# RWKV-6 scan and squared-ReLU MLP on one core: w in two-token rows for four chunks, the decay sum moved into the state update's bank, a split last tile, and a new order

## The chip, the cores and the metric

The kernel runs on one core of a Trainium2 chip. Five queues run side by side, each in its own order: TensorE (PE), VectorE (DVE), ScalarE (ACT), GpSimd (POOL) and SyncE (SP), which here only starts DMA transfers. The metric is the device time of one execution in microseconds, as the median of several runs.

## The reference

Four sequences, eight heads, 768 tokens, 48 channels per head. A linear recurrence with a decay `w` per channel and token is followed by a two-layer MLP over all 3072 tokens:

```
for t in range(S):
    cur = einsum('bhd,bhe->bhde', u[None] * kt, vt)
    y[:, :, t] = einsum('bhd,bhde->bhe', rt, state + cur)
    state = wt[:, :, :, None] * state + einsum('bhd,bhe->bhde', kt, vt)
x = y.transpose(0, 2, 1, 3).reshape(B * S, H * D)      # 3072 x 384
r = maximum(x @ w_in, 0.0)                             # w_in 384 x 2048
out = (r * r) @ w_out                                  # w_out 2048 x 384
```

## The kernel before

**Tiling.** The tokens are cut into 24 chunks ("steps") of 128 tokens, six for each sequence. A step is done for all eight heads at once, tokens on the partitions. The MLP works on 12 blocks of two steps each: `m1` is the first layer (a group `m1:i:g` makes two of the 16 slices of 128 hidden channels, 6 matmuls of 256 columns), `rl` the ReLU on ACT, `gt` the square on DVE, `m2` the second layer (a quarter `m2:i:mt:q` is 4 matmuls of 384 columns, and four quarters make an output tile of 128 tokens), `os` its copy out of PSUM, `store` the transfer out.

**One step of the scan.** `ld` brings r, k, v and w of the step, each one transfer of 192 KB. `lw` takes the logarithm of w on ACT. `cum` is a matmul with a triangular matrix, which sums the logarithms over the tokens into a tile `cp` of two PSUM banks. `exp` turns it into decay factors on ACT, and `rd` multiplies r and k with them on DVE. `tr` and `rkt` transpose the result (PE, then DVE), `p` and `pm` make the masked scores, `su` the chunk's contribution to the state, `ts` adds it to the state (DVE), and `sn` multiplies the state with the decay of the whole chunk, `a_c` (POOL). `y` makes the outputs, `ku`, `qp`, `q`, `vq` the term with `u`, `ysb` adds it, and `yt` and `xt` transpose into `xT`, the input of the MLP.

**What the change touches.** `a_c` needs the sum of the logarithms over the chunk. Five small matmuls put it beside the running sum, in the bank of `cp` (lines 190 to 195), and ACT takes its exponential at the end of `exp` (lines 207 to 209). For the first `V5 = 8` steps `cum` has a second matmul with a negated triangular matrix (line 198), and `exp` is one activation of 768 elements (line 203). Later steps use only the first matmul, two activations of 384 (lines 205 and 206), and the pair `rw` (ACT, line 160) and `kw` (POOL, line 164), which rescales k.

**PSUM.** There are eight banks: `cp` has two and is used in turn by `cum` and `p`; `y` has one; `tr` has one, which is used in turn by the transposes of `tr`, by `su` and by `yt`; four `mm` banks are for the MLP and for `warm`, matmuls on zeros that compute nothing.

**The order.** Everything is put into its queue by a list of words written out by a planner beforehand, `order`, that is read from left to right. A word such as `su:4` puts the instructions of `su` for step 4 into the queues. Within an engine the order of the list holds; between engines semaphores do the waiting. The list begins so:

```python
    order = """
        ld:0:w ld:0:r warm:6:0 ld:1:w ld:0:k lw:0 ld:0:u cum:0 ld:0:v warm:4:1 ld:1:v lw:1 ld:1:r exp:0 ub ld:1:k rd:0
        ...
```

`warm:6:0` is six matmuls into bank 0. `ld:n:I` and `ld:n:O` are the eighths of the two MLP weight matrices (384 KB each, lines 90 and 96); `cast` copies them into bf16 (line 104), even groups on ACT and odd groups on DVE.

Of the kernel before, what the change touches and what calls it, by code (L numbers as in the profile page):

```python
# [16 lines left out]
def kernel(  # L17
# [11 lines left out]
    nc = tc.nc  # L29
# [14 lines left out]
    A_IN = 7  # L44

# [26 lines left out]
    def load_step(step, part):  # L72
        b, c = divmod(step, NCH)
        if part in "wv":
            raw[part, step] = a_in.tile([C, H, D], FP32, name=part + "_raw")
            load_one(raw[part, step][:], w if part == "w" else v, b, c)
        else:
            if ("rk", step) not in raw:
                raw["rk", step] = a_in.tile([C, 2, H, D], FP32, name="rk_raw")
            i = "rk".index(part)  # L80
            load_one(raw["rk", step][:, i], (r, k)[i], b, c)
# [26 lines left out]
    u_row = consts.tile([1, H, D], FP32)  # L108
# [3 lines left out]
    def load_u():  # L112
        nc.sync.dma_start(out=u_row[:], in_=u[None])

    def ub_():
        ps = tiles["ub"] = ps_y_pool.tile([C, H, D], FP32, name="y")
        nc.tensor.matmul(ps[:], ones_row[:], u_row[:], start=True, stop=True)
# [3 lines left out]

    tri_strict = consts.tile([C, C], BF16)
# [14 lines left out]
    V5 = 8  # L137
    NLW = 3
# [15 lines left out]
    def lw_(s):  # L154
        lw = tiles["lw", s] = lw_bufs[s % NLW]
        nc.scalar.activation(lw[:, :, 0:D], raw["w", s][:], AF.Ln)  # L156
# [43 lines left out]
    def exp_(s):  # L200
# [6 lines left out]
        if s % NCH < NCH - 1:  # L207
            a_c = tiles["a_c", s] = a_small.tile([C, HP, 2], FP32, name="a_c")
            nc.scalar.activation(a_c[:], cs[:, 0, DM:DM + 2 * HP].rearrange("p (a e) -> p a e", e=2), AF.Exp)  # L209
# [18 lines left out]
    def p_(s):  # L228
        rkT = tiles["rkT", s]
        ps_p = tiles["p", s] = ps_cp.tile([C, 2, 512], FP32, name="cp")  # L230
        for p in range(HP):
            for e in range(2):
                rows = slice(e * DP, (e + 1) * DP)
                nc.tensor.matmul(ps_p[:, e, p * C:(p + 1) * C], rkT[rows, 1, p, :],  # L234
                                 rkT[rows, 0, p, :], start=True, stop=True)
# [7 lines left out]

    def su_(s):
        rdec, v_bf = tiles["rdec", s], tiles["v", s]
        ps_su = tiles["su", s] = ps_tr_pool.tile([C, HP, 2, D], FP32, name="tr")
        for p in range(HP):
            nc.tensor.matmul(ps_su[:, p], rdec[:, 1, 2 * p:2 * p + 2, :],
                             v_bf[:, 2 * p:2 * p + 2, :], start=True, stop=True)

    def ts_(s):
        ps_su = tiles.pop(("su", s))
        ts = tiles["ts", s] = a_mid.tile([C, HP, 2, D], FP32, name="t_state")
        if s % NCH == 0:
            nc.vector.tensor_copy(ts[:], ps_su[:])
        else:
            nc.vector.tensor_add(ts[:], tiles["S", s][:], ps_su[:])  # L257
# [76 lines left out]

    def warm_(n, b):
# [4 lines left out]
    def ld_(n, x):  # L340
        {"i": load_wi, "o": load_wo}.get(x.lower(), lambda g: load_u() if x == "u" else load_step(g, x))(n)

    run = dict(rw=rw_, kw=kw_, lw=lw_, v=v_, cum=cum_, exp=exp_, rd=rd_, tr=tr_, rkt=rkt_, p=p_, pm=pm_, su=su_, ts=ts_,
# [4 lines left out]
        ld:0:w ld:0:r warm:6:0 ld:1:w ld:0:k lw:0 ld:0:u cum:0 ld:0:v warm:4:1 ld:1:v lw:1 ld:1:r exp:0 ub ld:1:k rd:0  # L348
        warm:1:2 uc ld:2:w cum:1 v:0 ku:0 exp:1 su:0 ld:3:w warm:3:3 ts:0 v:1 tr:0 sn:0 ld:2:v warm:9:0 rd:1 ku:1 ld:2:r
        rkt:0 qp:0 lw:2 ld:2:k p:0 qp:1 tr:1 pm:0 ld:0:I warm:4:1 ld:3:r ld:4:w rkt:1 cum:2 y:0 exp:2 su:1 ld:3:k  # L350
        warm:10:2 ts:1 v:2 q:1 sn:1 rd:2 ku:2 ld:3:v q:0 cast:i:0:0 p:1 su:2 vq:0 pm:1 warm:5:3 lw:3 ld:1:I ld:2:I qp:2
        ld:3:I ts:2 cum:3 ld:4:I ysb:0 vq:1 tr:2 exp:3 ld:4:r y:1 rkt:2 ku:3 ld:4:v warm:1:0 rd:3 yt:0 warm:3:1 xt:0
        qp:3 ysb:1 lw:4 tr:3 sn:2 v:3 p:2 rkt:3 warm:2:2 pm:2 yt:1 ld:5:I warm:4:3 xt:1 cast:i:0:1 cast:i:1:0 p:3 ld:6:I
        y:2 q:2 m1:0:0:0 pm:3 vq:2 ld:4:k cast:i:2:0 m1:0:2:1 su:3 rl:0:0 ld:5:w ysb:2 m1:0:4:2 ts:3 v:4 cum:4 q:3
        ld:7:I yt:2 rl:0:4 m1:0:1:3 vq:3 exp:4 y:3 ld:0:O sn:3 warm:3:0 ysb:3 ld:1:O xt:2 cast:i:1:1 rl:0:2 ld:2:O yt:3
        warm:1:2 ld:3:O m1:0:3:0 xt:3 rd:4 ku:4 ld:6:w cast:i:2:1 m1:1:4:2 ld:4:O qp:4 rl:0:1 su:4 ld:5:k m1:1:5:1 lw:5
        gt:0:0 m1:0:5:3 rl:0:3 ts:4 rl:1:4 m1:1:2:0 gt:0:1 rl:1:5 m1:1:0:2 cast:i:3:1 rl:0:5 tr:4 cast:i:3:0 rl:1:2
        m1:1:3:1 rkt:4 ld:5:r cast:o:0:1 m1:0:6:3 gt:0:2 p:4 rl:1:3 m1:1:1:0 cast:o:1:0 rl:1:0 m1:1:6:1 pm:4 rl:1:1
        ld:5:O m1:1:7:2 cast:o:0:0 ld:6:O gt:1:2 y:4 lw:6 ld:7:O m1:0:7:0 gt:1:0 rl:0:6 cum:5 gt:1:1 rl:0:7 ld:6:k
        m2:0:0:0:3 exp:5 cast:o:1:1 m2:0:1:0:0 ld:6:r q:4 rl:1:6 m2:0:0:1:3 vq:4 rd:5 cast:o:2:0 m2:0:1:1:0 ld:5:v ku:5  # L360
        m2:1:1:0:1 m2:1:1:1:1 gt:0:3 cast:o:2:1 sn:4 tr:5 cum:6 qp:5 rkt:5 m2:0:1:2:0 exp:6 cast:o:3:0 m2:0:0:2:3 ld:7:w
        cast:o:3:1 rl:1:7 m2:1:1:2:1 ku:6 q:5 ld:6:v m2:0:0:3:3 rd:6 m2:0:1:3:0 ld:7:k os:0:0 ysb:4 vq:5 tr:6 ld:7:r p:5
        rkt:6 m2:1:0:0:2 qp:6 lw:7 ld:7:v pm:5 yt:4 v:5 m2:1:0:1:2 os:0:1 ld:8:w xt:4 gt:1:3 cum:7 v:6 y:5 q:6 ld:8:k
        exp:7 su:6 ysb:5 m2:1:1:3:1 vq:6 ts:6 ld:8:r m2:1:0:2:2 os:1:1 rd:7 sn:6 yt:5 v:7 m2:1:0:3:2 ld:9:k xt:5 ku:7
        p:6 lw:8 su:7 ld:9:w pm:6 m1:2:6:3 rw:8 qp:7 m1:2:0:0 os:1:0 ld:9:r rl:2:6 ts:7 cum:8 ku:8 y:6 exp:8 tr:7 ld:8:v
        ysb:6 kw:8 m1:2:7:1 rkt:7 rl:2:0 ld:10:k m1:2:1:2 sn:7 rd:8 rl:2:7 yt:6 m1:2:2:3 ld:10:r ku:9 lw:9 q:7 p:7 xt:6
        m1:2:4:0 ld:11:k pm:7 qp:9 rl:2:2 m1:2:3:1 rl:2:1 ld:10:w vq:7 m1:2:5:3 q:9 v:8 rw:9 gt:2:0 tr:8 ld:9:v cum:9
        rl:2:3 kw:9 rkt:8 y:7 rl:2:4 ld:11:w m2:2:1:0:2 gt:2:1 exp:9 qp:8 su:8 ysb:7 m2:2:0:0:1 store:0:0 ts:8 ld:10:v
        m2:2:0:1:1 ku:10 rl:2:5 rd:9 ld:11:r yt:7 lw:10 m2:2:1:1:2 xt:7 vq:9 q:8 cum:10 ld:12:w rw:10 tr:9 gt:2:2 exp:10
        m1:3:0:0 kw:10 rkt:9 m2:2:0:2:1 ld:12:k v:9 sn:8 m1:3:1:3 rd:10 rl:3:0 ld:13:w m2:2:1:2:2 ku:11 lw:11 m1:3:4:0  # L370
        rl:3:1 ld:14:w gt:2:3 p:9 vq:8 rl:3:4 m1:3:6:3 pm:9 ld:12:r lw:12 qp:10 su:9 m2:2:0:3:1 v:10 ld:13:r gt:3:0 p:8
        os:2:0 m1:3:2:0 ku:12 ts:9 rw:12 ld:11:v m1:3:3:1 pm:8 rl:3:2 sn:9 su:10 rw:11 m1:3:5:0 ld:14:r lw:13 kw:11
        ts:10 y:8 rl:3:5 store:2:0 tr:10 ysb:8 store:1:0 sn:10 rl:3:6 cum:11 ld:13:k rkt:10 m1:3:7:0 exp:11 qp:11
        ld:14:k m2:3:1:0:3 q:10 rl:3:3 ld:12:v rd:11 y:9 qp:12 yt:8 m2:2:1:3:2 xt:8 gt:3:1 cum:12 v:11 kw:12 tr:11 ysb:9
        exp:12 ld:15:k m2:3:0:0:1 gt:3:2 m2:3:1:1:3 rkt:11 rl:3:7 ld:15:w m2:3:0:1:1 os:2:1 rd:12 ku:14 yt:9 ld:16:k
        rw:13 m2:3:1:2:3 xt:9 vq:10 p:11 lw:14 ld:16:w m2:3:0:2:1 pm:11 rw:14 ku:13 m1:4:2:0 ld:15:r m1:4:4:2 q:11
        rl:4:2 ld:17:k p:10 gt:3:3 v:12 y:11 vq:11 rl:4:4 pm:10 m2:3:0:3:1 ld:18:k lw:15 qp:13 m1:4:0:0 os:3:0 ysb:11
        ld:19:k m1:4:1:2 kw:13 rl:4:0 q:13 yt:11 y:10 q:12 rl:4:1 ld:13:v cum:13 xt:11 qp:14 ysb:10 m1:4:3:1 exp:13
        store:0:1 yt:10 gt:4:0 ld:14:v m1:4:6:0 ld:15:v q:14 xt:10 m1:4:5:2 rd:13 rl:4:3 m2:3:1:3:3 store:1:1 rl:4:5
        ld:16:r su:12 cum:14 v:13 ts:12 m1:5:6:1 os:3:1 gt:4:1 ld:20:k tr:12 rl:5:6 sn:12 m1:4:7:2 rkt:12 lw:16 ld:17:w  # L380
        ku:16 m1:5:0:3 rl:4:6 m1:5:2:1 gt:4:2 rl:4:7 kw:14 su:13 exp:14 ld:17:r m2:4:1:0:0 gt:4:3 m2:4:0:0:2 ld:18:w
        ku:15 rl:5:0 m2:4:0:1:2 ts:13 rl:5:2 rd:14 m1:5:3:3 ld:19:w sn:13 rw:16 tr:13 rl:5:3 kw:16 ld:16:v cum:16 rkt:13
        m2:4:0:2:2 exp:16 qp:15 m1:5:1:1 ld:18:r m1:5:7:3 rd:16 ku:17 ld:17:v m2:4:1:1:0 rl:5:7 gt:5:1 p:13 rw:15
# [68 lines left out]
```

## Time and profile before

| what | value |
|---|---|
| median of 11 runs | 198.14 us (196.70 to 198.99) |
| the profiled execution's own time | 198.69 us |
| its span in the profile | 196.9 us |
| PE busy | 188.5 us, 96% of the span |
| DVE, ACT, POOL busy | 144.4, 131.6, 109.6 us |
| HBM traffic | 29.9 MB, of which 4.7 MB written |
| packets under 512 bytes | 100481 of 108696 |

The profile is of one execution. Its span is 1.8 us shorter than its own time, which also has what lies before the first and behind the last recorded instruction. [...]a busy PE row doesn't tell how much of the time was needed.

### The profile page before, as it was taken

The numbers are of one execution on the slowest core, as the hardware profiler recorded it, in microseconds if no ns is written. First come the engines' busy times: TensorE is split into PE (matmuls) and PEld (weight loads), VectorE is DVE, ScalarE is ACT, GpSimd is POOL, SyncE is SP. The second block draws the span as 40 slices with busy tenths as digits, with TensorE's granted clock in tenths as the row PEclk, the third lists the DMA queues.
The fourth block names the chain that finished last, engine by engine and source line by source line (L and its number), as shares of the span: only waits on it lengthen the run. The fifth ranks groups of instructions, "written<-read, shape, count | busy, mean of one in ns | idle before, by whom it ended". The sixth has DMA issues, their size and how long they took to land.

```text
span 196.9 us, 4956 instructions
## 1 busy us (share of the span) xinstructions
PE 188.5 (96%) x1954; PEld 136.2 (69%) x1958; DVE 144.4 (73%) x202; ACT 131.6 (67%) x278; POOL 109.6 (56%) x124
## 2 busy tenths in 40 slices
PE   7999978999999999999999999999999999999992
PEld 2355555876678767678776778877777778778650
DVE  3369776997878979997969886977897885844210
ACT  3625658894788878878975767678776568438221
POOL 6278634127489999973995299430999390010000
PEclk9999999999999999999999999999999999999999
DMA  6999889999979999999985097705730000015013
GB/s 132 217 235 221 263 236 218 351 260 255 220 157 220 201 212 255 181 223 221 213 177 122 3 200 202 159 4 139 166 62 0 3 0 2 3 40 203 0 40 120
DMA packets 108696, 30.20 MB, mean 153 GB/s; under 512 B 100481, under 2 KB 108674, under 8 KB 108674
## 3 DMA queue, kind: packets, MB, share of 16 engines
q1 hardware_dynamic: 108674, 29.89, 65.6%
q8 instruction: 15, 0.25, 0.5%
q14 instruction: 7, 0.06, 0.1%
HBM read 25.17 MB, written 4.72 MB: 152 GB/s over the span
## 4 chain that ended last, share of the span: by engine, by line
PE 68%; SPq 9%; DVE 7%; DMA 6%; POOL 4%; ACT 2%; issue 2%; DVEq 0%; POOLq 0%; ACTq 0%
PE mm L324 27%; PE mm L300 26%; SPq L67 7%; PE tr L222 4%; DMA w_st<-in_moe_w_in_dram 4%; PE cp L234 3%; DVE gt L317 2%; PE y L269 2%; DMA v_raw<-in_v_dram 2%; DVE pmT L239 2%; SPq L90 2%; PE tr L285 2%; PE cp L196 1%; DVE rdec_buf L213 1%; PE y L274 1%
## 5 line engine op out<-in xcount | busy, mean ns | idle before, releaser
L300 PE MATMUL mm<-xT,wi_sb 128*128 128x256 bf16 x576 | 72.7, 273 | 1.5 <-ACT wi_sb L104 1.2
L324 PE MATMUL mm<-wo_sb,gt 128*128 128x384 bf16 x384 | 71.6, 326 | 0.0
L309 ACT ACTIVATE rl<-mm 128x512 f16<-128x512 f32 x96 | 55.8, 598 | 20.3 <-PE mm L300 15.1
L300 PEld LDWEIGHTS <-wi_sb 128*128 128x128 bf16 x576 | 54.1, 98 | 11.3 <-ACT wi_sb L104 1.3
L324 PEld LDWEIGHTS <-gt 128*128 128x128 bf16 x384 | 35.8, 98 | 19.0
L317 DVE TENSOR_TENSOR gt<-rl 128x1024 bf16<-128x1024 f16 x48 | 41.0, 870 | 9.4 <-ACT rl L309 9.4
L261 POOL TENSOR_TENSOR S<-t_state,a_c 128x384 bf16<-128x384 f32 x20 | 17.7, 885 | 30.1 <-DVE t_state L257 16.4
L184 POOL TENSOR_TENSOR vq<-v_raw,q 128x384 f32<-128x384 f32 x24 | 22.8, 954 | 17.5 <-DVE q L180 15.4
L239 DVE TENSOR_TENSOR pmT<-cp,tri_strict 128x1024 bf16<-128x1024 f32 x24 | 29.2, 1218 | 4.5 <-PE cp L234 4.3
L172 POOL TENSOR_TENSOR ku<-rk_raw,u_bc 128x384 f32<-128x384 f32 x24 | 25.1, 1048 | 8.8 <-ACT u_bc L120 4.4
L213 DVE TENSOR_TENSOR rdec_buf<-rk_raw,cp 128x768 bf16<-128x768 f32 x24 | 22.8, 950 | 9.6 <-ACT a_c L209 5.5
L176 POOL TENSOR_TENSOR qprod<-rk_raw,ku 128x384 f32<-128x384 f32 x24 | 25.4, 1064 | 0.5
L226 DVE COPY rkT<-tr 128x1024 bf16<-128x1024 bf16 x24 | 16.5, 687 | 9.0 <-PE tr L222 8.8
L164 POOL TENSOR_TENSOR rk_raw<-rk_raw,rw 128x384 f32<-128x384 f32 x16 | 18.2, 1136 | 5.9 <-ACT rw L160 5.8
L329 ACT ACTIVATE o_sb<-mm 128x384 f32<-128x384 f32 x24 | 11.6, 491 | 9.7 <-PE mm L324 9.7
L288 ACT COPY xT<-tr 128x384 bf16<-128x384 bf16 x24 | 11.5, 479 | 9.8 <-PE tr L285 9.5
L338 PE MATMUL mm<-warm 128*128 128x512 bf16 x52 | 16.2, 428 | 1.5 <-DVE ones L132 1.3
L279 DVE TENSOR_TENSOR y_sb<-vq,y 128x384 bf16<-128x384 f32 x24 | 13.2, 548 | 4.6 <-PE y L274 4.1
L156 ACT ACTIVATE lw_buf<-w_raw 128x384 bf16<-128x384 f32 x24 | 12.4, 521 | 4.9 <-DMA w_raw<-in_w_dram 4.9
L222 PE MATMUL tr<-ident,rdec_buf 128*128 128x128 bf16 x192 | 14.6, 219 | 0.1
L222 PEld LDWEIGHTS <-rdec_buf 128*128 128x128 bf16 x192 | 12.3, 98 | 2.3 <-issue 0.5
L180 DVE TENSOR_REDUCE q<-qprod 128x8 f32<-128x384 f32 x24 | 13.0, 544 | 0.2 <-POOL qprod L176 0.2
(53 smaller groups left out, 178.7 us busy)
## 6 DMA issues: line engine op xcount, KB each, us to landing
w_raw<-in_w_dram SPq DMA_DIRECT2D x24, 192.0 KB, 3.8
rk_raw<-in_r_dram SPq DMA_DIRECT2D x24, 192.0 KB, 3.6
rk_raw<-in_k_dram SPq DMA_DIRECT2D x24, 192.0 KB, 3.8
v_raw<-in_v_dram SPq DMA_DIRECT2D x24, 192.0 KB, 4.0
out_dram<-o_sb SPq DMA_DIRECT2D x24, 192.0 KB, 2.1
w_st<-in_moe_w_in_dram SPq DMA_DIRECT2D x8, 384.0 KB, 5.2
w_st<-in_moe_w_out_dram SPq DMA_DIRECT2D x8, 384.0 KB, 5.5
u_row<-in_u_dram SPq DMA_DIRECT2D x1, 1.5 KB
```

The costliest lines, as they stand in the source:

```text
L164: nc.gpsimd.tensor_mul(k_s, k_s, tiles.pop(("rw", s))[:])
L172: nc.gpsimd.tensor_mul(ku[:], raw["rk", s][:, 1], u_bc[:])
L176: nc.gpsimd.tensor_mul(qp[:], raw["rk", s][:, 0], tiles.pop(("ku", s))[:])
L184: nc.gpsimd.tensor_mul(vq[:], raw["v", s][:], tiles.pop(("q", s))[:, :, None].to_broadcast([C, H, D]))
L213: nc.vector.tensor_mul(rdec[:, :, :, 0:D], raw["rk", s][:], tiles.pop(("cs", s))[:, :, 0:DM].rearrange("p a (h d) -> p a h d", h=H))
L222: nc.tensor.transpose(ps_tr[:, i, p, :], rdec[:, i, 2 * p:2 * p + 2, :], ident[:])
L239: nc.vector.tensor_mul(pmT[:].rearrange("p e a t -> p (e a) t"), tiles.pop(("p", s))[:].rearrange("p e (a t) -> p (e a) t", a=HP), tri_str ...
L261: nc.gpsimd.tensor_mul(S[:], tiles.pop(("ts", s))[:], tiles.pop(("a_c", s))[:, :, :, None].to_broadcast([C, HP, 2, D]))
L300: nc.tensor.matmul(ps1[:, j * width:(j + 1) * width], wi_sb[:, kk, n * 128:(n + 1) * 128], xT[:, kk, s0 * C:s0 * C + width], start=(kk == ...
L309: nc.scalar.activation(tiles["rl", i, q][:, j], tiles.pop(("m1", i, g))[:], AF.Relu, scale=RS)
L317: nc.vector.tensor_mul(tiles["gt", i][:, 4 * q:4 * q + 4, :].rearrange("p a b -> p (a b)"), rl, rl)
L324: nc.tensor.matmul(tiles["m2", i, mt][:, 0:DM], gt[:, n, mt * 128:(mt + 1) * 128], wo_sb[:, n, :], start=(n == 0), stop=(n == NT - 1))
```

## The change

1. **Two-token rows.** For steps 0 to 3 (`WIDE = 4`), w is loaded by two transfers of 64 partitions. The first 64 partitions hold four heads, the others the other four heads, and each row has two consecutive tokens side by side, so that a contiguous piece is 384 bytes and not 192. `lw` reorders while it takes the logarithm, and `cum` is eight matmuls of 192 columns with two new matrices `tri_pair` in place of two of 384. The setup of these matrices adds a memset and two selects on POOL and a multiplication on DVE.
2. **The decay sum beside the state.** The five small matmuls move from `cum` to the end of `su` and write the bank `tr`. For steps 0 to 3 they are nine. The activation becomes a word of its own, `ac`.
3. **The last tile.** The 16 matmuls of 384 columns of the last output tile become two times 16 of 192; the first half is copied out by ACT and the second by DVE, each with its own transfer.
4. **Constants.** `V5` goes from 8 to 5, so steps 5 to 7 take the path with `rw` and `kw`. `NLW`, the number of `lw` buffers, goes from 3 to 4. `u_row` lies in row 0 of `u_bc`. The function `pmh_` and the argument `banks` of `p_` are new in the file, but no word uses them.
5. **The order** is written anew throughout, on all queues, the transfers too. `warm` matmuls go from 56 to 45.

```diff
         if part in "wv":
             raw[part, step] = a_in.tile([C, H, D], FP32, name=part + "_raw")
-            load_one(raw[part, step][:], w if part == "w" else v, b, c)
+            if part == "w" and step < WIDE:
+                for g in range(2):
+                    nc.sync.dma_start(
+                        out=raw[part, step][g * 64:(g + 1) * 64].rearrange("p (h f) d -> p h (f d)", f=2),
+                        in_=w[b, g * 4:(g + 1) * 4, c * C:(c + 1) * C, :].rearrange("h (p f) d -> p h (f d)", f=2))
+            else:
+                load_one(raw[part, step][:], w if part == "w" else v, b, c)
...
+    tri_pair = [consts.tile([C, 2, C + 2], BF16, name=f"tri_pair{i}") for i in range(2)]
...
-    V5 = 8
-    NLW = 3
+    V5 = 5
+    NLW = 4
...
-        if s % NCH < NCH - 1:
-            nc.tensor.matmul(cs[:, 0, DM:DM + 2 * HP], ident[:], other_head[:], start=True,
-                             stop=False, skip_group_check=True)
-            for p in range(HP):
-                nc.tensor.matmul(cs[:, 0, DM + 2 * p:DM + 2 * p + 2], lw[:, 2 * p:2 * p + 2, :],
-                                 ones2[:], start=False, stop=True, skip_group_check=True)
+        if s < WIDE:
+            for i in range(2):
+                for g in range(2):
+                    for f in range(2):
+                        x = 1 + i - f
+                        nc.tensor.matmul(cs[:, i, g * DM // 2:(g + 1) * DM // 2], tri_pair[i][:, g, x:x + C],
+                                         lw[:, 4 * f:4 * f + 4, 0:D], start=(f == 0), stop=(f == 1))
+            return
...
+    def ac_(s):
+        a_c = tiles["a_c", s] = a_small.tile([C, HP, 2], FP32, name="a_c")
+        nc.scalar.activation(a_c[:], tiles["su", s][:, DM:DM + 2 * HP].rearrange("p (a e) -> p a e", e=2), AF.Exp)
...
     def su_(s):
...
+        nc.tensor.matmul(ps_su[:, DM:DM + 2 * HP], ident[:], other_head[:], start=True,
+                         stop=False, skip_group_check=True)
+        for p in range(HP):
+            halves = [(2 * p, ones2[:])]
+            if s < WIDE:
+                halves = [(4 * f + 2 * (p % 2), half_ones[:, p // 2]) for f in range(2)]
+            for h, one in halves:
+                nc.tensor.matmul(ps_su[:, DM + 2 * p:DM + 2 * p + 2], lw[:, h:h + 2, :],
+                                 one, start=False, stop=(h == halves[-1][0]), skip_group_check=True)
...
+    def last_(i, mt, b, j):
+        gt, cols = tiles["gt", i], slice(j * DM // 2, (j + 1) * DM // 2)
+        ps, o_sb = bank(b), o_pool.tile([C, DM], FP32, name="o_sb")
+        for n in range(NT):
+            nc.tensor.matmul(ps[:, 0:DM // 2], gt[:, n, mt * 128:(mt + 1) * 128], wo_sb[:, n, cols],
+                             start=(n == 0), stop=(n == NT - 1))
+        if j == 0:
+            nc.scalar.activation(o_sb[:, cols], ps[:, 0:DM // 2], AF.Copy, scale=1.0 / (RS * RS))
+        else:
+            nc.vector.tensor_scalar_mul(o_sb[:, cols], ps[:, 0:DM // 2], 1.0 / (RS * RS))
+        t0 = (blocks[i][0] + mt) * C
+        nc.sync.dma_start(out=out[t0:t0 + C, cols], in_=o_sb[:, cols])
...
     order = """
-        ld:0:w ld:0:r warm:6:0 ld:1:w ld:0:k lw:0 ld:0:u cum:0 ld:0:v warm:4:1 ld:1:v lw:1 ld:1:r exp:0 ub ld:1:k rd:0
-        warm:1:2 uc ld:2:w cum:1 v:0 ku:0 exp:1 su:0 ld:3:w warm:3:3 ts:0 v:1 tr:0 sn:0 ld:2:v warm:9:0 rd:1 ku:1 ld:2:r
...
-        m1:11:3:2 m2:10:1:2:1 rl:11:3 m2:11:0:0:3 os:10:0 gt:11:1 m2:10:1:3:1 store:10:0 m2:11:1:0:2 m2:11:0:1:3
-        m2:11:0:2:3 m2:11:0:3:3 m2:11:1:1:2 os:11:0 m2:11:1:2:2 os:10:1 store:10:1 m2:11:1:3:2 store:11:0 os:11:1
-        store:11:1
+        ld:0:r ld:0:w warm:7:0 ld:0:u ld:0:k ld:0:v ld:1:w lw:0 ld:1:k cum:0 ub ld:1:r exp:0 ld:2:w warm:2:1 v:0 rd:0
+        lw:1 ld:0:I ld:3:w uc cum:1 ku:0 tr:0 ld:2:k exp:1 ld:1:v warm:4:2 rkt:0 ku:1 rd:1 su:0 qp:0 warm:2:3 ac:0
+        ld:2:r ts:0 p:0 q:0 tr:1 cast:i:0:0 ld:4:w warm:6:0 pm:0 lw:2 ku:2 ld:5:w lw:3 rkt:1 cum:2 vq:0 ld:2:v y:0 exp:2
+        warm:4:1 qp:1 ysb:0 ld:1:I v:1 rd:2 yt:0 ld:3:r warm:3:2 qp:2 xt:0 ld:3:k lw:4 q:1 tr:2 sn:0 p:1 rkt:2 ld:2:I
+        warm:2:3 vq:1 pm:1 su:1 warm:3:0 ld:3:I ac:1 v:2 ts:1 p:2 lw:5 ld:4:I y:1 sn:1 rw:5 pm:2 ld:3:v su:2 warm:2:1
+        ld:5:I ac:2 ysb:1 cum:3 ku:3 ts:2 warm:1:2 ld:4:r exp:3 q:2 yt:1 sn:2 y:2 warm:2:3 xt:1 rd:3 vq:2 m1:0:0:0 tr:3
...
+        os:10:1 m2:11:0:3:2 store:10:1 os:11:0 store:11:0 last:11:1:3:0 last:11:1:0:1
```

## The prediction

> **What bounds the kernel now.** First the table of busy times and the slices of the page:
>
> ```profile
> PE 188.5 (96%) x1954; PEld 136.2 (69%) x1958; DVE 144.4 (73%) x202; ACT 131.6 (67%) x278; POOL 109.6 (56%) x124
> ...
> PE   7999978999999999999999999999999999999992
> ...
> DMA  6999889999979999999985097705730000015013
> ```
>
> PE is the fullest engine, and its row has nines nearly to the end. But `warm` counts as busy, so this row says nothing about the ramp. I cut the span at the first group of `m1` (24.76 us), the first of `m2` (42.05) and the end of the last matmul (193.14), and took busy times by stage:
>
> ```profile
> 0.00:24.76 24.76, 22.70 (x193) 11.33 (x197) 15.36 (x25) 12.11 (x23) 14.86 (x29) 1.00 0.95 214
> 24.76:42.05 17.29, 15.23 (x166) 12.04 (x165) 14.51 (x22) 13.23 (x25) 4.79 (x5) 1.00 0.96 264
> 42.05:193.14 151.09, 150.59 (x1601) 112.86 (x1598) 114.54 (x157) 105.80 (x230) 90.00 (x90) 1.00 0.59 131
> ```
>
> (Columns: stage, length, busy PE, weight load, DVE, ACT, POOL; clock, DMA share, GB/s.) In the last stage PE is never out of work and the transfers have slack. In the first two the transfers are full (0.95, 0.96). The chain of waits says the same and shows the tail:
>
> ```profile
> 19.34 7.53 DMA w_st<-in_moe_w_in_dram
> ...
> 26.89 0.84 ACT wi_sb L104
> ...
> 27.77 0.83 PE mm L300 x6
> ...
> 193.16 0.49 ACT o_sb L329
> ```
>
> The third `m1` group waits for a `cast`, which waits for an eighth of `w_in` that lands at 26.86. So the end is: a ramp set by the transfers and by the scan's first chain through DVE, then PE's whole remaining work without a gap, then 3.8 us of copy and store.
>
> To see what PE really needs I use the spacing of matmuls in that chain, not their durations: an `m1` group of six takes 0.65 us, four of 384 columns 0.65, `tr` 0.45, `p` 0.33, `y` 0.20 and 0.18 more for the state, `su` 0.18, `yt` 0.17, a 384-column matmul of `cum` 0.163, the five small ones 0.11, a `warm` 0.213. Summed over the words of the order before: 18.4 us up to the first `m1` (11.1 of them `warm`), 14.3 between the first `m1` and the first `m2`, 147.4 from there. Against the stage lengths PE lost 6.4, 3.0 and 3.7 us. The last stage has little to give.
>
> **What the Trainium skill says.** "DMA: Bandwidth & Descriptors", Why small descriptors are slow: each packet pays about 3 bus cycles beside one per 32 bytes, and carries fixed metadata; Specifications gives 512 bytes as the least for full rate. The trace agrees in kind: the stretch from 4 to 12 us, all 192-byte pieces, moved 224 GB/s. The same page's Rules for kernel authors say that two transfers to the two halves of the partitions share the same engines and gain nothing by being two; no run here shows it yet. "TensorE: Matmul & The Clock Gate", Back-to-back issue gap, gives N/2.4 + 2.5 ns: 162.5 for 384 and 109 for 256, as the trace has them, so I take 82 ns for the new 192-column matmuls, an estimate from that page.
>
> **The change part by part.**
>
> *Wide w.* A 192 KB transfer took 196.6 KB / 224 GB/s = 0.88 us. With half as many pieces it takes 0.44 if the cost is by the piece; by the page's cycles, 15 per 384 bytes against 2 x 9, it takes 0.73. That saves 0.15 to 0.44 each, 0.6 to 1.8 us over four; below nothing if the second issue on SP (0.4 to 0.9 us each before) held up the queue, which I exclude, because SP is already ahead of the transfers: its issue at 13.57 takes 2.2 us, waiting for an older one to land. For the first load there is a loss: r now goes before w. So w:0 lands at 3.42 + 0.44 to 0.73, and `lw:0` starts 0.4 to 0.8 later than 3.46. PE pays: `cum` for four steps is 8 x 0.082 = 0.66 instead of 0.33, +1.3 us, and `su` gets 16 small matmuls more, +0.4 at 0.025 each. Both lie in the ramp, where `warm` stood. The first `cum` runs at the cold clock and costs 1.3 us.
>
> *a_c out of `exp`.* The timeline at the start:
>
> ```profile
> 5.75 0.52 ACT L156 ACTIVATE lw_buf<-w_raw 128x384 bf16<-128x384 f32 x1 [1.76 <-DMA w_raw<-in_w_dram]
> 6.18 0.79 ACT L203 ACTIVATE cp<-cp 128x768 f32<-128x768 f32 x1
> 7.00 0.18 ACT L209 ACTIVATE a_c<-cp 128x8 f32<-128x8 f32 x1
> 7.21 0.95 DVE L213 TENSOR_TENSOR rdec_buf<-rk_raw,cp 128x768 bf16<-128x768 f32 x1 [4.33 <-ACT a_c L209]
> ```
>
> Here `exp:0` stood behind `lw:1`, which waited for the second w, and `rd:0` stood behind `a_c`, 0.2 us. The new list has `exp:0` before `lw:1`, and `a_c` later. So `rd:0` starts at 4.0 (w lands, mean) + 0.52 + 1.3 + 0.25 + 0.8 = 6.9 instead of 7.2. From there DVE carries the chain. Up to `ysb:1` it has three `rd` (0.95), three `rkt` (0.69), two `ts` and two `q` (0.55), three `pm` (1.22) and one `ysb` (0.55): 11.3 us, where before it had four `rd`, three `ts` and two `pm`: 11.6 us in 14.2. With the same 2.5 idle, `ysb:1` starts at 20.7 (before 21.37), then `ysb`, `ts:2`, `yt:1` and `xt:1` (0.55 + 0.55 + 0.35 + 0.48) let the first `m1` start at 22.7; the sum of PE's words gives 16.1 + 6.4 = 22.5. Before: 24.76. The 20 activations stay 0.18 each.
>
> *V5.* Steps 5 to 7 lose a 384-column matmul (-0.5 us PE) and get `rw` (0.53 ACT), `kw` (1.14 POOL), two exps (0.96) for one (0.80). That is +2.1 ACT and +3.4 POOL. The second stage covers POOL's (4.8 busy of 17.3) and most of ACT's (13.2 busy). Without that cover `rd:5` would come up to 1.1 us later.
>
> *The order.* Eleven `warm` fewer, -2.3 us. New sums: 16.1, 15.2 and 147.7 us against 18.4, 14.3 and 147.4. So PE's list is 1.1 us shorter in all, provided it idles as before. The transfers: `ld:1:O`, which the first `m2` now needs, is the end of the first 8.45 MB and not 8.06, +1.7 us at 235 GB/s (8.06 MB between 2.75 and 37.1 us, when its `cast` starts); the wide rows give back 0.6 to 1.8. The first `m2` is thus due at about 40.5 by the transfers and at 22.6 + 15.2 + 2 to 3 = 40.3 by PE; before 42.05. The setup (a few hundred ns on POOL and DVE) hides behind the first transfer; it costs up to 0.3 us if `lw_buf`'s memset ends behind w:0.
>
> *The tail.* Two times 16 x 0.082 = 2.6 us is what the 16 matmuls took. The last copy is 192 columns on DVE: by L213 (768: 0.95) and L255 (384: 0.56) some 0.36 instead of 0.49. The last store has half the bytes: 0 to 0.4 less of 2.1. Together -0.15 to -0.5, I take -0.35.
>
> *The sum.* -1.1 for PE's list, -0.5 for less idling in the ramp (0 to -1.2: the transfers' gain less what `ld:1:O` loses), -0.35 for the tail, +0.25 for waits of the new order in the long stage (0 to +3; it lost 3.7 before): **-1.7**. From the profiled 198.69 this makes 197.0; that execution lies 0.55 above the median of 198.14, so I forecast **196.5**.
>
> **Rivals.** Half a per cent, 1.0 us, is about what a measurement of this kernel can tell from no change.
>
> *No gain (0.20).* Pieces of 384 bytes cost by the byte, w:0 comes late behind r, `ld:1:O` lands 1.7 later, and only the list's surplus and the tail remain, partly eaten: -0.6, 197.5. For it speaks that stage two was already full of transfers; against it, that 192-byte pieces run at 224 GB/s while stage two, with larger ones among them, runs at 264.
>
> *Slower: the `tr` bank (0.22).* One bank serves `tr`, `su` and `yt`. It came free when DVE had done `ts`; now ACT must also have done `ac`, and ACT is in order. While it is held, PE stands at the next `tr` or `yt` with all of the MLP behind it. By the new list, PE has 1.3 to 3.3 us of other work between `su` and that point in 18 of 20 cases, but in eight ACT has one to three activations of 0.5 to 0.6 us before `ac`. ACT can be late: before, `sn` on POOL once waited 7.0 us for the activation of L206, just ahead of `a_c`. At 0.2 us for each of the 20 the price is 4 us: 198.14 - 1.7 + 4 = 200.4. It decides from (1.7 + 1.0) / 20 = 0.14 us per step. Against it: the median cover of 1.9 us.
>
> *A larger gain.* If pieces cost by the number, the ramp idles 1.2 us less and the long stage nothing more: 195.2; counted with my forecast, 0.58 together.
>
> **The numbers.** My case reaches from 194.6 (1.2 from the ramp, a tail of -0.5, a part of PE's 3.7 us of loss gone) to 197.2. The range takes in no gain and the milder half of the slow case: 194.6 to 199.6. Faster 0.58, within 0.5% 0.20, slower 0.22.
>
> **What would show it.** Right: first `m1` at 22 to 23.5, first `m2` at 39.5 to 41, a last stage of 151 to 152 us, the last copy at 0.36 us on DVE, 4 to 12 us at more than 224 GB/s. Wrong: PE waiting for `ac` at the next `tr` or `yt`; a last stage over 153 us; a first `m1` after 24.

## The result, and the profile after

The changed kernel took **200.07 us** (median; 199.46 to 201.94), the kernel before 197.83 on the same chip: a ratio of 1.0125, 95% interval [1.010, 1.015]. A copy of it on another chip gave 1.0092 [1.0057, 1.0126]. It is slower by about 1%, and outside my range of 194.6 to 199.6 us.

The profile after, in the order in which that of before was read: busy times and slices of the page, then the three stages cut at the first `m1`, the first `m2` and the end of the last matmul (columns as before).

```profile
PE 189.4 (95%) x1996; PEld 139.1 (70%) x2000; DVE 145.2 (73%) x207; ACT 132.5 (67%) x284; POOL 113.8 (57%) x131
...
PE   6999988969999999999999999999999999999993
...
DMA  4999999999999999999999997040380001001422
```

```profile
0.00:25.45 25.45, 22.88 (x194) 13.13 (x198) 14.64 (x28) 11.54 (x22) 15.15 (x32) 1.00 1.02 192
25.45:44.52 19.07, 16.14 (x179) 12.82 (x180) 15.19 (x22) 14.62 (x28) 9.88 (x11) 1.00 1.08 276
44.52:195.16 150.64, 150.36 (x1625) 113.19 (x1622) 115.06 (x158) 106.38 (x235) 88.80 (x90) 1.00 0.67 132
```

The first slice of DMA is 4 where it was 6, and the first stage moved 192 GB/s where it moved 214. The stages took 25.45, 19.07 and 150.64 us; before it was 24.76, 17.29 and 151.09. So in these two profiles the loss is in the first two stages, 2.5 us, and the long stage gave back 0.45. In the copies of both kernels on another chip (`b0_same`, `a0_same`, below) the first `m1` is at 24.92 and 26.01 and the first `m2` at 43.26 and 44.49: the loss ahead of the first `m2` is there too, but it is 1.2 us. Where the loss lies is thus known, and its size by stage only within about 1 us.

The start, from the timelines of ACT, DVE and PE (start, duration, engine, line, and in brackets the idle time before it and what ended it):

```profile
4.67 0.52 ACT L176 ACTIVATE lw_buf<-w_raw 128x384 bf16<-128x384 f32 x1 [2.65 <-POOL lw_buf L161]
6.72 0.80 ACT L228 ACTIVATE cp<-cp 128x768 f32<-128x768 f32 x1 [1.53 <-PE cp L218]
...
8.68 0.52 ACT L176 ACTIVATE lw_buf<-w_raw 128x384 bf16<-128x384 f32 x1 [0.47 <-DMA w_raw<-in_w_dram]
...
7.55 0.95 DVE L238 TENSOR_TENSOR rdec_buf<-rk_raw,cp 128x768 bf16<-128x768 f32 x1 [4.35 <-ACT cp L228]
11.59 0.69 DVE L251 COPY rkT<-tr 128x1024 bf16<-128x1024 bf16 x1 [3.08 <-PE tr L247]
...
9.26 1.44 PE L218 MATMUL cp<-lw_buf,tri_pair 128*128 128x192 bf16 x8
10.49 1.06 PE L247 MATMUL tr<-ident,rdec_buf 128*128 128x128 bf16 x8
```

`rd:0` starts at 7.55. Then DVE stands 3.08 us until `tr:0` is there, because on PE `tr:0` is behind `cum:1`, and `cum:1` starts only as `lw:1` ends (9.20), which waited for the second w. Both are slow, too: 1.44 us for matmuls that take 0.82 in step 2 (16.35), and 1.06 for transposes that take 0.61 four microseconds later. `cum:0` also took 1.44 us here, and 0.82 in the copy `a0_same`: the speed of these early matmuls differs between two executions of the same kernel. Ahead of `lw:0` the profile names POOL, which sets an `lw` buffer (line 161); in `a0_same`, where `lw:0` starts at 5.05, it names w itself.

The chain of waits in the second stage, and the last copy:

```profile
30.70 5.96 DMA rk_raw<-in_k_dram
...
36.78 1.00 POOL ku L195
...
37.86 1.33 POOL rk_raw L187
...
39.22 0.95 DVE rdec_buf L238
...
40.95 0.69 DVE rkT L251
...
41.68 0.61 PE tr L247 x8
```

```profile
195.16 0.36 DVE L391 TENSOR_SCALAR o_sb<-mm 128x192 f32<-128x192 f32 x1 [5.97 <-PE mm L386]
```

The k of step 5 lands at 36.66; `ku:5`, `kw:5`, `rd:5` follow, and `rkt:4`, long ready, is behind `rd:5` in DVE's queue, so PE stands 1.5 us ahead of `tr:5`. PE waits for the `tr` bank, which `ac` and `ts` hold, only 0.2 us in all; DVE waits 2.7 us for `ac`.

### The profile page after: what moved, and what is told of

It reads as the page before. It is cut to its first block, busy times and chain, and to the rows that moved or that the text cites. A ratio compares the mean times of both kernels' runs of the same rounds, so it can differ in the third digit from the quotient of the medians.

```text
span 198.4 us, 5067 instructions
## 1 busy us (share of the span) xinstructions
PE 189.4 (95%) x1996; PEld 139.1 (70%) x2000; DVE 145.2 (73%) x207; ACT 132.5 (67%) x284; POOL 113.8 (57%) x131
## 3 DMA queue, kind: packets, MB, share of 16 engines
q1 hardware_dynamic: 106834, 29.89, 73.9%
## 4 chain that ended last, share of the span: by engine, by line
PE 76%; SPq 14%; DMA 3%; DVE 1%; issue 1%; POOL 1%; ACT 0%; ACTq 0%; POOLq 0%
PE mm L371 30%; PE mm L347 28%; SPq L68 8%; PE tr L247 4%; PE cp L265 3%; SPq L97 3%; DMA rk_raw<-in_k_dram 3%; SPq L79 3%; PE y L316 2%; PE tr L332 2%; PE cp L221 2%; PE y L321 1%; PE tr L286 1%; PE mm L386 1%; PE tr L295 1%
## 5 line engine op out<-in xcount | busy, mean ns | idle before, releaser
L347 PE MATMUL mm<-xT,wi_sb 128*128 128x256 bf16 x576 | 74.5, 273 | 0.2 <-DVE wi_sb L111 0.2
L371 PE MATMUL mm<-wo_sb,gt 128*128 128x384 bf16 x368 | 70.3, 326 | 0.0
L356 ACT ACTIVATE rl<-mm 128x512 f16<-128x512 f32 x96 | 55.1, 597 | 18.2 <-PE mm L347 17.2
L371 PEld LDWEIGHTS <-gt 128*128 128x128 bf16 x368 | 33.9, 98 | 17.3 <-issue 0.2
L207 POOL TENSOR_TENSOR vq<-v_raw,q 128x384 f32<-128x384 f32 x24 | 21.5, 895 | 25.6 <-DVE q L203 25.6
L199 POOL TENSOR_TENSOR qprod<-rk_raw,ku 128x384 f32<-128x384 f32 x24 | 26.1, 1090 | 2.3 <-DMA rk_raw<-in_r_dram 2.0
L187 POOL TENSOR_TENSOR rk_raw<-rk_raw,rw 128x384 f32<-128x384 f32 x19 | 21.4, 1127 | 8.5 <-ACT rw L183 8.3
L247 PEld LDWEIGHTS <-rdec_buf 128*128 128x128 bf16 x192 | 12.9, 100 | 4.4 <-issue 2.1
L398 PE MATMUL mm<-warm 128*128 128x512 bf16 x41 | 14.1, 458 | 1.7 <-DVE warm L148 1.3
L191 ACT CAST v_bf<-v_raw 128x384 bf16<-128x384 f32 x24 | 12.2, 509 | 1.4 <-PE y L316 1.2
```

The source lines that it names most:

```text
L187: nc.gpsimd.tensor_mul(k_s, k_s, tiles.pop(("rw", s))[:])
L199: nc.gpsimd.tensor_mul(qp[:], raw["rk", s][:, 0], tiles.pop(("ku", s))[:])
L207: nc.gpsimd.tensor_mul(vq[:], raw["v", s][:], tiles.pop(("q", s))[:, :, None].to_broadcast([C, H, D]))
L247: nc.tensor.transpose(ps_tr[:, i, p, :], rdec[:, i, 2 * p:2 * p + 2, :], ident[:])
L347: nc.tensor.matmul(ps1[:, j * width:(j + 1) * width], wi_sb[:, kk, n * 128:(n + 1) * 128], xT[:, kk, s0 * C:s0 * C + width], start=(kk == ...
L356: nc.scalar.activation(tiles["rl", i, q][:, j], tiles.pop(("m1", i, g))[:], AF.Relu, scale=RS)
```

## Experiments

All ratios are to the kernel before on the same chip, with a 95% interval; 1% is 2 us. Three theories were set against each other first. *Supply*: the wide loads make the early transfers slower. *Order*: the new list waits where the old one did not, at `rd:5` above all. *PE work*: the eight matmuls of `cum` and the nine small ones cost their time.

**Plain w in the changed kernel.** `e1_narrow` has the old `cum` too, `e2_plain_load` only the old loads.

```diff
-    WIDE = 4
+    WIDE = 0                                    # e1_narrow
-            if part == "w" and step < WIDE:
+            if part == "w" and step < 0:        # e2_plain_load
```

> The changed kernel with WIDE = 0: w is loaded plainly, four issues fewer on SP, cum is two matmuls of 384 again and su has five small ones; order, V5 and the rest as changed. Three theories. Supply: each half load of w holds SP's queue as long as a whole one (0.60 to 1.03 us against 0.43 to 0.58 for the r, k and v between them), the transfers starve in the first 10 us (167 and 178 GB/s from 4 to 8 us against 222 and 229), and the 0.45 MB missing at 16 to 36 us is about 2 us for everything behind: without the wide loads 0.2 to 0.25 MB comes back and the time falls by 1 to 2.5 us, to 197.6 to 199.1. Order: the wait of PE at 40 to 42 us and the later ones come from the new queues, not from the loads: within 0.7 of the changed kernel's 200.1. PE work: the 1.7 us that wide cum and su add are paid once PE is full, and only that comes back: 198.4, with the first m1 where it was.

> The changed kernel with only the loads of w for steps 0 to 3 made plain; lw, cum and su still treat the rows as two-token rows, so the decay sums mix other tokens than they should, and all instructions outside SP are the same. Supply: 1 to 2 us faster than the changed kernel (198.1 to 199.1), GB/s from 4 to 8 us back at 200 or more, first m1 before 24.8. PE work: no change. Order: no change, within 0.5. If 384-byte pieces do save transfer time, this one is slower than the changed kernel by up to 1 us.

Measured: 1.0054 [1.0032, 1.0076] and 1.0070 [1.0046, 1.0093]. Plain loads alone bring the ratio from 1.0125 (1.0092 in the copy) to 1.0070, which is a quarter to a half of the loss; the wide `cum` adds 0.16% in this order, less than the intervals can tell; half a per cent is elsewhere. From 4 to 8 us `e2_plain_load` moved 196 GB/s (the changed kernel 173) and its first `m1` came at 25.00, both short of what *Supply* had asked for.

**V5 back to 8.**

```diff
-    V5 = 5
+    V5 = 8      # and rw_, kw_ return at once for s < V5
```

> The changed kernel with V5 = 8 as before: steps 5 to 7 have the second matmul of cum and one exp, and no rw and kw. Order theory: rkt:4 stands behind rd:5 on DVE, rd:5 waited until 39.22 us for kw:5 on POOL, which waited for k of step 5 (landed 36.7); PE stood at tr:5 till 41.7. Without kw, rd:5 is ready when k lands, about 2 us earlier, less 0.5 us of PE for the three matmuls: 1 to 1.5 us faster, 198.6 to 199.1. Supply: k of step 5 still lands late, so at most 1 us comes back. PE work: 0.5 us slower.

Measured: 1.0113 [1.0079, 1.0147], between the two ratios of the changed kernel. `kw:5` lies in the chain, yet without it nothing is gained.

**The wide path in the order before.** Loads, `lw`, `cum` and the small matmuls of the change, the sum left in `cp`'s bank, all else as before.

```diff
+    WIDE = 4    # load_step, lw_, cum_ as in the change; halves/half_ones in cp's bank
```

> The kernel before with the wide loads alone (two half loads of w, lw reordering, wide cum, nine small matmuls for steps 0 to 3, in cp's bank as before; the setup of the new matrices; the row of u in u_bc). Order list unchanged. Supply: slower than the kernel before by 1 to 2.5 us (SP starts everything after the first w later by 0.2 to 0.6 us per half load, four times). My prediction's step (a gain of 0.6 to 1.8 us in the transfers): as fast or faster, -1 to +0.3. PE work alone: +0.3 to +1.7.

Measured: 1.0137 [1.0094, 1.0179], first `m1` at 29.30 us (before 24.76). I had set 1.7 us of PE's work, covered by `warm`, against 0.6 to 1.8 of gain; it loses 2.7 us by itself, a little more than the 1 to 2.5 of *Supply*.

**Copies and the tail alone.** `b0_same` is the kernel before, one execution; `a0_same` the changed kernel; `b_last` the kernel before with its last output tile in two halves.

```diff
-        ... m2:11:1:0:2 ... m2:11:1:1:2 os:11:0 m2:11:1:2:2 os:10:1 store:10:1 m2:11:1:3:2 store:11:0 os:11:1 store:11:1
+        ... os:11:0 os:10:1 store:10:1 store:11:0 last:11:1:2:0 last:11:1:0:1      # b_last
```

> A copy of the kernel before, for a profile on the same chip as the others of this call. All theories: the time of the kernel before. The transfers' rate is open: the profile of the kernel before moved 222 GB/s of 192-byte pieces from 4 to 8 us, while in the four kernels tried so far plain pieces ran at 180 to 205. If this copy has about 190, the slower transfers belong to the chip and not to the change; if 220, to the new order.

> A copy of the changed kernel, as the reference for this call. 1.0125 of the kernel before, as measured; first m1 0.7 us later and first m2 2.5 us later than in the copy of the kernel before if the two profiles compared so far were of like chips; if the chips differed, both differences shrink.

> The kernel before with the last tile in two halves alone. My prediction's step: 0.15 to 0.5 us faster. The changed kernel's profile has the last copy at 0.36 us on DVE and 3.26 us from the last matmul's end to the end of the span, against 3.76 before: 0.4 us faster, ratio 0.998. Rival: the end of the span is set by the fixed time of a transfer, so nothing: 1.000.

Measured: 199.93 us for `b0_same`, its span 198.2 against 196.9 on the first chip; so single profiles differ by over 1 us and only ratios carry small differences. From 4 to 8 us it moved 201 GB/s, between the 190 and the 220 that I had set for chip and order, so it decides nothing there. `a0_same` 1.0092 [1.0057, 1.0126], `b_last` 1.0008 [0.9987, 1.0028].

**The second half from ACT's queue.**

```diff
-                    nc.sync.dma_start(
+                    (nc.scalar if g and step else nc.sync).dma_start(
```

> The changed kernel with the second half load of w for steps 1 to 3 issued from ACT's queue instead of SP's; same transfers. Supply theory, in the form that SP's issue time is what costs: three issues of 0.6 to 1.0 us leave SP, everything behind them starts up to 2 us earlier, 0.6 to 1.4 us faster than the copy of the changed kernel. In the form that the pieces of half the partitions themselves move slowly: no gain, since the transfers are the same. Either way ACT pays up to 0.6 us each where it isn't idle.

Measured: 1.0116 [1.0080, 1.0152], no gain; by the expectation that speaks against the issue time. It is not a clean test, though: the timelines of ACT and its queue show that the edit also brought w:1's half ahead of w:0, first here, then in the changed kernel on the same chip (`a0_same`).

```profile
0.76 0.69 ACTq L79 DMA_DIRECT2D w_raw<-in_w_dram  x1
...
5.32 0.52 ACT L176 ACTIVATE lw_buf<-w_raw 128x384 bf16<-128x384 f32 x1 [3.31 <-DMA w_raw<-in_w_dram]
```

```profile
5.05 0.52 ACT L176 ACTIVATE lw_buf<-w_raw 128x384 bf16<-128x384 f32 x1 [3.03 <-DMA w_raw<-in_w_dram]
```

`lw:0` starts 0.27 us later than in that copy, and 0.65 later than in the first profile of the changed kernel (4.67). The k of step 2 is issued 1.5 us earlier (9.20, not 10.72), and yet the first `m1` is at 25.89 (26.01). So this run neither confirms the issue time nor rules it out. A run that moves a cost to another queue must be read for what it moved with it.

**Pieces against halves, in the order before.** The two parts of the wide load, apart and together, nothing else changed (the code is shortened). `b_pieces` reads four heads of 256 tokens, so it and `b_2x384` compute with the w of other tokens and heads; the instructions are the same.

```diff
+ for g in range(2): ... out=raw[g*64:(g+1)*64], in_=w[b, :, c*C+g*64:c*C+(g+1)*64, :]     # b_split: 2 x 64 partitions, 192 B
+ out=raw (p (h f) d), in_=w[b, g:g+4, t:t+2*C, :] "h (p f) d -> p h (f d)"              # b_pieces: 1 x 128 partitions, 384 B
+ the two transfers of the change                                                        # b_2x384: 2 x 64 partitions, 384 B
```

> The kernel before, with one edit: w of steps 0 to 3 comes as two transfers of 64 partitions each, still in 192-byte pieces (same bytes, same layout, same number of pieces). Half-partition theory (two issues for half a partition range each are slow, whatever the pieces): 201 to 202.5 us, ratio 1.010 to 1.017, first m1 two to four us later than before. Piece theory (the 384-byte pieces are what is slow): ratio 0.998 to 1.003. Work theory (the eight matmuls of the new cum and its reordered lw cost the time): 0.998 to 1.003.

> The kernel before, with one edit: w of steps 0 to 3 is one transfer of all 128 partitions in 384-byte pieces (four heads, 256 tokens; so the decays are those of other tokens and heads, which changes no instruction's time). Half the pieces, one issue. Half-partition theory: the saving that I predicted shows, ratio 0.990 to 0.999, first m1 up to 1 us earlier. Piece theory: ratio 1.007 to 1.015. Work theory: 0.990 to 1.000.

> The kernel before, with the two half-partition transfers of 384-byte pieces for w of steps 0 to 3 and nothing else of the change (lw and cum stay as before and so mix tokens and heads, which changes no instruction's time). Half-partition theory and piece theory: ratio 1.010 to 1.014, nearly all of the 1.0137 of the kernel that has the new cum too. Work theory: 0.998 to 1.004.

| w of steps 0 to 3 | one transfer | two transfers |
|---|---|---|
| 192-byte pieces | 1 (before) | 1.0063 [1.0036, 1.0091] |
| 384-byte pieces | **0.9941 [0.9920, 0.9961]** | 1.0048 [1.0020, 1.0076] |

Larger pieces save 1.2 us, as I had worked out. The second transfer costs 1.3 us with small pieces and 2.1 with large ones; the two runs with two transfers lie below the 1.010 that the half-partition theory asked for at least, and above what its rivals asked for. Where the time goes is seen in SP's own queue (start, duration; x2 is two issues in a row), with large pieces, first one transfer, then two:

```profile
0.74 0.42 SPq L78 DMA_DIRECT2D w_raw<-in_w_dram  x1
...
1.76 0.57 SPq L78 DMA_DIRECT2D w_raw<-in_w_dram  x1
...
7.15 1.31 SPq L78 DMA_DIRECT2D w_raw<-in_w_dram  x2
8.51 0.51 SPq L67 DMA_DIRECT2D v_raw<-in_v_dram  x1
```

```profile
0.73 1.38 SPq L78 DMA_DIRECT2D w_raw<-in_w_dram  x2
...
2.81 1.25 SPq L78 DMA_DIRECT2D w_raw<-in_w_dram  x2
...
8.64 2.69 SPq L78 DMA_DIRECT2D w_raw<-in_w_dram  x4
11.38 0.60 SPq L67 DMA_DIRECT2D v_raw<-in_v_dram  x1
```

The tile of w in the second kernel has eight issues with 595/615/718 ns (least, median, most): an issue for half the partitions takes as long as one for all (423/540/766 in the first). SP comes to v of step 2 at 11.38 and not at 8.51. The other explanation would be that transfers to half the partitions are slow themselves. Against it, the first w land 3.1 us after their issue in the median (3.6 with one transfer, of twice the bytes), and all transfers together took 65.0% of the time of the 16 DMA engines (66.1). Two transfers over all 128 partitions, which would separate the two for good, were not run. Meanwhile the DMA engines get less to do. From 8 to 14 us (columns as in the stages), with one transfer, then with two:

```profile
8.00:14.00 6.00, 5.74 (x53) 3.02 (x52) 3.43 (x5) 2.46 (x6) 4.70 (x5) 1.00 1.11 235
```

```profile
8.00:14.00 6.00, 5.40 (x28) 2.73 (x28) 3.16 (x4) 3.06 (x8) 3.81 (x5) 0.52 0.91 192
```

192 GB/s against 235, and PE, starved, was granted half the clock in this execution (0.52). The clock isn't the cause of the longer time: in the five executions of `b_2x384` whose mean clock was under 0.99 the median is 199.6 us, in the twelve at 0.996 or more 199.7.

**One transfer in the changed kernel.** The decisive run: the same edit, with all of the change beside it.

```diff
-                for g in range(2):
-                    nc.sync.dma_start(out=raw[part, step][g * 64:(g + 1) * 64]...
+                g, t = (c % 2) * 4, (c // 2) * 2 * C
+                nc.sync.dma_start(out=raw[part, step][:]..., in_=w[b, g:g + 4, t:t + 2 * C, :]...
```

> The changed kernel with one edit: w of steps 0 to 3 is one transfer of all 128 partitions in 384-byte pieces and not two of 64 partitions (other tokens and heads, so the decays mix; no other instruction changes). Second-issue theory, from the 2.1 us between the two forms in the order of before (1.0048 against 0.9941): 0.7 to 1.1% less than the changed kernel, so a ratio of 0.998 to 1.004. If in the new order the form of these loads matters little, as the run with half of them issued by ACT hinted: 1.006 to 1.012.

Measured: 1.0013 [0.9996, 1.0030] against 1.0125 and 1.0092. The second transfer is 0.8 to 1.1% of the changed kernel's time, most of what it loses. With one transfer and large pieces it is also faster than with plain w (1.0071 on the same chip), which fits the saving of `b_pieces`. SP's queue, in the changed kernel, then with one transfer:

```profile
1.22 1.36 SPq L79 DMA_DIRECT2D w_raw<-in_w_dram  x2
...
4.24 1.69 SPq L79 DMA_DIRECT2D w_raw<-in_w_dram  x2
...
7.24 1.50 SPq L79 DMA_DIRECT2D w_raw<-in_w_dram  x2
...
9.44 1.26 SPq L79 DMA_DIRECT2D w_raw<-in_w_dram  x2
10.74 0.60 SPq L68 DMA_DIRECT2D rk_raw<-in_k_dram  x1
```

```profile
1.22 0.57 SPq L79 DMA_DIRECT2D w_raw<-in_w_dram  x1
...
3.32 1.41 SPq L79 DMA_DIRECT2D w_raw<-in_w_dram  x1
...
6.02 1.25 SPq L79 DMA_DIRECT2D w_raw<-in_w_dram  x1
...
7.86 0.49 SPq L79 DMA_DIRECT2D w_raw<-in_w_dram  x1
8.39 0.51 SPq L68 DMA_DIRECT2D rk_raw<-in_k_dram  x1
```

The k of step 2 is issued 2.35 us earlier; from 4 to 12 us the transfers moved 238 GB/s (200, in `a0_same` too); the first `m1` is at 24.11 (25.45 and 26.01), the first `m2` at 42.26 (44.52 and 44.49). `rd:0` starts at 6.82 (7.55 and 7.31), but that is hardly the loads: `lw:0` starts 0.11 us earlier than in the first profile, and 0.62 is `cum:0`, which took 0.82 us and not 1.44.

**What else the change costs: the decay sum.** `b_ac` puts it beside the state in the order before; `a_cp` puts it back in the changed kernel with plain w.

```diff
-    NLW = 3
+    NLW = 5      # b_ac: sum in su's bank, ac:s ahead of each ts:s, lw:19 and rw:19 behind su:14
-    ac:0 ... ac:22
+    (none)       # a_cp: WIDE = 0, sum in cp's bank, a_c at the end of exp
```

> The kernel before, with the decay sum beside the state alone: five small matmuls at the end of su in the bank of tr, the word ac just ahead of each ts, five lw buffers, and lw:19 and rw:19 moved behind su:14 to let the buffer come free. If the held tr bank costs what my slower rival said: 0.1 to 0.2 us for each of 20 steps, ratio 1.010 to 1.020. If it is free, as the waits of the changed kernel say: 0.997 to 1.003; then what is left of the change beside the wide loads is the order.

> The changed kernel with plain w (WIDE = 0) and the decay sum put back: the five small matmuls in the bank of cp, its activation at the end of exp, no ac words; so what is left of the change is the order, V5, NLW and the split tile. Theory that the decay sum beside the state costs: 0.997 to 1.002, against the 1.0054 with the sum beside the state. Theory that the order costs: 1.004 to 1.008.

Measured: `b_ac` 1.0140 [1.0102, 1.0177], `a_cp` 1.0091 [1.0055, 1.0127]. In the old order the held bank does cost: PE's waits there

```profile
PE tr L217 <- DVE t_state L257: 1.4, 3, 0.8
...
PE tr L217 <- DVE t_state L255: 0.6, 1, 0.6
```

are new, four of them, 2.0 us in all (columns: total, times, longest); DVE waits 12.7 us for `ac` there. The run also has five `lw` buffers and two moved words, so not all of its loss need be the bank. In the new order PE's waits are gone (0.2), and taking the sum back gains nothing.

**The sequence of loads, and one word.** `a_ldorder` sets the loads in the old sequence into the new order, with plain w; `a_narrow2` is `e1_narrow` once more beside it. `n_rkt` (plain w) and `a_rkt` (wide w) move the word that stood behind `rd:5`.

```diff
-        ... rd:5 cast:i:3:0 m1:1:5:2 qp:5 rkt:4 warm:1:3
+        ... rkt:4 rd:5 cast:i:3:0 m1:1:5:2 qp:5 warm:1:3      # n_rkt, a_rkt
```

> The changed kernel with plain w (WIDE = 0) and the loads in the sequence of the order before, set into the places of the new order's loads (10 of 113 sooner where a use asks for it). Theory that the new sequence of the loads costs in the first 45 us: 0.998 to 1.003. Theory that the sequence of the computing words or ac costs: 1.004 to 1.010; it may also be worse than the 1.0054 of the same kernel with its own sequence, where the computing words wait for loads that they were planned around.

> The changed kernel with plain w (WIDE = 0), once more, on the chip of the two runs beside it, to compare them with: 1.003 to 1.008, as in its first run (1.0054), by every theory.

> The changed kernel with plain w (WIDE = 0) and rkt:4 moved ahead of rd:5 in DVE's queue, one word. In the trace DVE waits for rd:5 (for the k of step 5, through POOL) with the finished transposes of step 4 behind it, and PE stands 1.0 us at tr:5. Theory that this wait is most of what the new order costs: tr:5 starts 0.9 to 1.5 us earlier, PE's wait at it is under 0.3 us, ratio 0.999 to 1.003 against 1.0054 and 1.0071 without the edit. Theory that the time is lost elsewhere and PE is made to wait again later: 1.004 to 1.008.

> The changed kernel with that one word moved and wide w kept. PE's wait at tr:5 was 1.5 us. First theory: ratio 1.003 to 1.007, against 1.0092 and 1.0125 without the edit. Second theory: 1.008 to 1.013.

Measured: `a_ldorder` 1.0758 [1.0722, 1.0793], worse than either theory said: the computing words are planned around their loads, and one wait alone, at a `yt`, is

```profile
PE tr L332 <- DVE t_state L304: 7.2, 1, 7.2
```

so it says nothing on the new sequence as such. `a_narrow2` 1.0071 [1.0045, 1.0097]. `n_rkt` 1.0063 [1.0034, 1.0092] and `a_rkt` 1.0083 [1.0055, 1.0112], neither apart from the same kernel without the edit, although in the trace of `n_rkt` PE passes `tr:5` at once:

```profile
39.56 0.38 PE L398 MATMUL mm<-warm 128*128 128x512 bf16 x1
40.06 0.62 PE L247 MATMUL tr<-ident,rdec_buf 128*128 128x128 bf16 x8
```

That wait, the largest of PE's in the changed kernel behind the start, was worth nothing that can be measured.

## Why the prediction was wrong

**The step that failed** is in *Wide w*: "below nothing if the second issue on SP (0.4 to 0.9 us each before) held up the queue, which I exclude, because SP is already ahead of the transfers". I had read that from one issue at 13.57 us. Ahead of that place the lead is small: in the kernel before SP issues without a gap from 0.74 us on, 17 issues in 12.8 us, 0.75 us each, the shortest 0.43, so by their lengths it waits a little at most of them. With halves most issues are near their least, 0.6 us, so that for most of the first 13 us SP and not the engines sets the pace. Nor were the transfers "full" at 0.95 and 0.96: the share reaches 1.13 from 4 to 12 us before, and 1.39 in the changed kernel from 14 to 20. The excluded term measured +2.1 us in the old order and +1.6 to +2.2 in the new one. That two transfers cost this is shown by the runs; that it is the time of the issue is read from SP's queue. It is about half of the 3.9 us between my −1.7 and the measured +2.2; most of the rest is the −1.1 of PE's list and the −0.35 of the tail, which did not come (below). The Trainium skill names this limit ("Perfetto Trace Analysis", What "DMA-bound" means: an issuing engine whose track is solid with DMA slices is a bound of its own, beside the 16 engines); the trace of `b_2x384` agrees, with SP solid and the engines' share at 0.91 from 8 to 14 us. But SP is solid in the kernel before as well; what differs is that its issues are stretched there (0.75 us each) and the share is 1.13. The page I had quoted ("DMA: Bandwidth & Descriptors", Rules for kernel authors) says that two transfers to the halves gain nothing; here each second one costs 0.62 us of SP.

**The piece size** was right: 0.6 to 1.8 us for four loads, measured 1.2 (0.9941).

**PE's pay for the wide `cum`**, +1.3 and +0.4, I set against `warm` as free. In the new order it nearly was (0.16%). In the old one `b_wide` less `b_2x384` is 0.9%, 1.8 us, uncertain by about 1 us; that is the size of the pay, but the two differ in the speed of their transfers too (last section), so it isn't shown to be PE's.

**The start** was 0.65 late: `rd:0` at 7.55, not 6.9. `lw:0` started at 4.67, not about 4.0, 4.56 with one transfer and 4.92 to 5.00 with plain w, so the second transfer is hardly the reason; `cum:0`, costed at 1.3 us, took 1.44, and 0.82 in the copy.

**The chain to the first `m1`**: I kept DVE's idle time at the old 2.5 us between `rd:0` and `ysb:1`. By the same subtraction it was 4.4 (15.7 less 11.3). The recorded gaps are 3.08 ahead of `rkt:0`, 0.86 ahead of `ts:0`, which the profile puts to `ac`, 0.73 and 0.25. `ysb:1` came at 23.22, not 20.7. With one transfer it is still 3.8, and the slow `cum:1` and `tr:0` are there too (1.44 and 1.06 us), so most of it is not the second transfer's.

**PE's list, −1.1**: its length was no saving. The eleven `warm` went out of a stage where PE waits anyway: by the same sums PE idled 9.4 us up to the first `m1` (25.45 − 16.1), where it had idled 6.4. The long stage was better than forecast, 150.64 against 151 to 152. From 4 to 12 us the transfers moved 200 GB/s, where I had asked for more than 224.

**The first `m2`**, forecast at 40.3 to 40.5, came at 44.52: 2.9 of it from the late first `m1`, the rest in the second stage, 19.07 us against my 17.7 or so. `ld:1:O` was not what it waited for: PE had `m1` to do right up to it, from 42.55 us on.

**V5** was rightly costed at nothing, as far as 1.0113 tells. **The tail**: the last copy took 0.36 as forecast, but of −0.35 us nothing showed, with −0.3 to +0.6 by the interval.

**Rivals.** The slower one had the sign and nearly the number (200.4), by the wrong mechanism: the `tr` bank is a real cost where an order isn't made for it (`b_ac`), not here.

**What stays open.** With plain w the changed kernel is still 0.5 to 0.7% slower, 1.1 to 1.4 us, and none of it came back with V5, the decay sum or `rkt:4`; the tail alone cost nothing in the order before. Some 0.3 us of it lies outside the span: own time less span is 1.81 to 2.45 us, mean 2.05, in the eleven kernels that have the new order with its own loads, and 1.73 to 1.80 in the seven of the order before without `ac`; why, no run tells. The rest is spread over the first 44 us, where one profile each doesn't resolve it; the slower transfers of the last section are one candidate, and no run takes the new matrices out. No version that beats the kernel before follows: the one faster run, with a single transfer of 384-byte pieces, loads the w of other tokens, and a single transfer in the layout of the change was not tried.

## What to carry to other kernels

Count issues as well as bytes and pieces: in a start-up where the issuing queue has no gaps and its issues are near their least duration, a transfer split in two delays all that stand behind it, even when the pieces get better. Judge whether a queue is ahead at the place of the edit, not where it happens to wait later. Filler taken out of a stage that another resource sets is no saving, and a chain's wait that is removed counts only once the time has been measured again.

## What was not expected of the hardware

An issue on SP cost no less for 64 partitions than for 128: 615 ns in the median for half a w (595 least), beside 423 to 766 ns for a whole one in the same pieces.

And plain pieces moved more slowly even where nothing is wide: from 52 to 56 us 188 GB/s at an engine share of 1.25, where the kernel before moved 212 at 1.07; w landed 4.6 us after its issue in the median, before 3.8. It doesn't take the new order. For the same 29.9 MB the transfers took 65.0 to 66.2% of the engines' time in all seven kernels without the matrices `tri_pair` and `half_ones`, and 68.9 to 73.9% in all thirteen that have them, among them `b_wide` with the old order and `a_ldorder` with the old sequence of loads (one line each of four pages: DMA queue, packets, MB, share of 16 engines; before, `b_2x384`, `b_wide`, changed):

```profile
q1 hardware_dynamic: 108674, 29.89, 65.6%
...
q1 hardware_dynamic: 106690, 29.89, 65.0%
...
q1 hardware_dynamic: 106690, 29.89, 71.3%
...
q1 hardware_dynamic: 106834, 29.89, 73.9%
```

The matrices take 1048 bytes of every partition. Whether it matters where the other tiles then lie, and what the slower transfers cost in time, no run tells.

And the granted clock of the profile can stay at 1.00 while matmuls are slow: in the first stage of the changed kernel it does, over the 1.44 us of `cum:1`, where the same matmuls of step 2 took 0.82.
